# TensorE's products as one loop of seven passes behind an empty pass, with GpSimd passing on its waits

## Chip, cores and metric

The kernel runs on one NeuronCore of a Trainium2 chip. The metric is the device time of one execution in microseconds; the median of the runs shown is given, and durations of single steps come from one profiled execution.

## What is computed

One decoding step for 8 sequences: layer norm, attention with 32 query heads over 4 key/value heads, where only the last 1024 of 4096 cached positions count, a residual, a second layer norm and a gated feed-forward block, all in float32.

```python
def reference(A_x, A_k_cache, A_v_cache, A_wq, A_wo, B_x, B_w_gate, B_w_up, B_w_down):
    # x (8,1,1024), wq (1024,4096), k/v_cache (8,4,4096,128), wo (4096,1024)
    q = heads(layernorm(x) @ wq)                 # 32 heads of 128
    k, v = the last W = 1024 rows of the caches, each head for 8 query heads
    p = softmax(q k^T * 128 ** -0.5)
    h = x + heads_joined(p v) @ wo
    g, u = layernorm(h) @ w_gate, layernorm(h) @ w_up      # (8,1,3584)
    return h + (gelu(g) * u) @ w_down                      # w_down (3584,1024)
```

All weights and the used part of the caches are read once, some 111 MB; there are only 8 rows of activations, so each number that is read takes part in 8 products per head or token.

## The kernel before

Each stage streams its operand from HBM into one of two SBUF buffers of 64 KB per partition (`space`, two times `BUF`) and TensorE multiplies the small activations (stationary, 32 columns) with 512 columns of it at a time. Four such products stand next to each other on the array, one per group of 32 columns, and are summed in PSUM over the steps of the contraction. The loads follow each other on SyncE's queue in a fixed order: `wq` (two of 8 MB), the keys (two), the values (two), `wo` (two), gate and up in a first set of 2048 columns (two of 8 MB) and a second of 1536 columns (two of 6 MB), then `w_down`, 28 blocks of 128 rows in parts of 8, 8, 4, 4, 2 and 1 blocks (`PARTS`), the last block in two halves (`ENDS`). A load waits until the products on the buffer's last content are done (`free`, `used`), and is then queued behind the load that is still running.

`Flow.run` puts one instruction on an engine with the waits that it needs and lets it count up the engine's semaphore; `Flow.move` issues one DMA with a semaphore of its own; a wait that the engine has already made is left out. Every program line is unrolled: 479 matrix products and transposes are written out one after the other (helper lines L192 for transposes, L237 `wq`, L265 scores, L312 values, L340 `wo`, L351 the fold of four partial sums, L380 gate and up, L466 and L489 to L501 `w_down`).

Between two products stand VectorE's and ScalarE's steps: scale and transpose of q (L243, L248), softmax (L274 to L279), the weighting of the heads (L319, L322), residual and second layer norm (L354, L202 to L223), gelu and product (L390, L393). From block 19 of `w_down` the last 296 columns (`SIDE_COLS`) are not moved with their part but by eight small DMAs of four rows each into a tile of their own, `w_side` (L440), and multiplied by L476.

The end: `d1` (L480) copies the sum of all but the last two blocks out of PSUM, L489 multiplies block 26 and folds `d1`, L501 multiplies the two halves of block 27 as they land, ScalarE copies each half (L504), and two DMAs write the output.

## Time and profile before

| | |
|---|---|
| median of 3 runs | 265.19 us (265.16 to 265.31) |
| span of the profiled execution, first to last instruction | 264.1 us |
| what lies around the span, by the median | 1.1 us |
| TensorE busy with products | 142.2 us (54%) |
| TensorE instructions (products and weight loads) | 958 and 958 |
| moved by DMA | 111.4 MB, mean 422 GB/s |
| of it, code of the engines | 8 packets, some 0.12 MB |
| mean granted TensorE clock | 0.793 |

The page puts the busy shares of the engines first, then the span in 40 slices, the DMA queues, and the chain of work that ended last. A queue of the kind "instruction" moves an engine's own program. In the views by window the DMA share is the mean busy share of the 16 DMA engines; a packet is counted where it starts, so that in windows shorter than a packet the share tells how many packets start there, and at the end of the kernel, where packets are short, how many of the 16 engines are still busy.

### The profile page before, as it was taken

What the parts mean: (1) busy time and instruction counts of PE and PEld (TensorE: products, weight loads), DVE (VectorE), ACT (ScalarE), POOL (GpSimd) and SP (SyncE); (2) the same over time, 40 slices, a digit from 0 to 9 for tenths busy, and PEclk for the clock granted to TensorE, in tenths of its full rate; (3) what the DMA queues carried; (4) which work ended last, traced back from release to release, by engine and by line L of the source; (5) the groups of instructions that cost most, each with busy time, mean ns of one, the idle gap of its engine ahead of it and who ended that gap; (6) DMA issues with size and microseconds to landing.
All of it is one profiled execution on the core that took longest, in us unless ns stands there. A gap on an engine that the chain in (4) does not pass through costs nothing.

```text
span 264.1 us, 2072 instructions
## 1 busy us (share of the span) xinstructions
PE 142.2 (54%) x958; PEld 40.9 (15%) x958; DVE 23.3 (9%) x55; ACT 10.9 (4%) x17; POOL 5.5 (2%) x15
## 2 busy tenths in 40 slices
PE   0006905905905906907807507818609477589875
PEld 0002201201201301302202102212102111113122
DVE  0040000000020110110110100170000200000001
ACT  1020000000010020020000000020000000000000
POOL 8000000000000000000000000000000000000000
PEclk9999985865875975985956965975957959599999
DMA  8998999999899989999998999899998999999994
GB/s 318 481 437 357 476 476 390 407 466 466 347 466 466 459 347 466 459 407 417 447 466 367 469 437 466 377 447 457 429 419 387 476 402 427 417 462 409 410 413 181
DMA packets 3256, 111.44 MB, mean 422 GB/s; under 512 B 392, under 2 KB 648, under 8 KB 1072
## 3 DMA queue, kind: packets, MB, share of 16 engines
q1 hardware_dynamic: 3088, 111.22, 97.9%
q8 instruction: 7, 0.11, 0.2%
q10 hardware_dynamic: 160, 0.10, 0.1%
q14 instruction: 1, 0.01, 0.0%
HBM read 111.18 MB, written 0.13 MB: 421 GB/s over the span
## 4 chain that ended last, share of the span: by engine, by line
DMA 78%; PE 21%; SPq 0%; issue 0%; ACT 0%
DMA w<-gu 20%; DMA w<-wq 16%; DMA w<-v 11%; DMA w<-kt 11%; DMA w<-wo 11%; DMA w<-dn 9%; PE big L380 6%; PE tb L312 4%; PE tb L237 4%; PE ya L340 3%; PE big L265 3%; SPq L91 0%; PE acc L489 0%; ACT o_fin L504 0%; PE tb L489 0%
## 5 line engine op out<-in xcount | busy, mean ns | idle before, releaser
L380 PE MATMUL big<-w,ln_t 128*32 128x512 f32 x224 | 37.7, 752 | 19.8 <-DMA w<-gu 19.8
L265 PE MATMUL big<-w,qz 128*32 128x512 f32 x128 | 18.8, 753 | 18.3 <-DMA w<-kt 18.3
L340 PE MATMUL ya<-w,ot 128*32 128x512 f32 x128 | 17.9, 721 | 19.9 <-DMA w<-wo 19.9
L466 PE MATMUL ya<-w,at 128*32 128x512 f32 (+1 forms) x104 | 16.4, 591 | 3.2 <-DMA w<-dn 3.2
L380 PEld LDWEIGHTS big<-w,ln_t 128*32 128x32 f32 x224 | 9.2, 134 | 46.9 <-issue 24.9
L192 PE MATMUL ta<-ident,ln_xn 64*128 64x64 f32 x16 | 2.2, 318 | 24.4 <-DVE ln_xn L218 24.4
L312 PE MATMUL tb<-w,pt 128*32 128x512 f32 x64 | 9.9, 787 | 9.0 <-DMA w<-v 9.0
L312 PE MATMUL acc<-w,pt 128*32 128x512 f32 x64 | 9.4, 751 | 9.5 <-DMA w<-v 9.5
L237 PE MATMUL tb<-w,ln_t 128*32 128x512 f32 x64 | 9.8, 783 | 8.6 <-DMA w<-wq 8.6
L237 PE MATMUL acc<-w,ln_t 128*32 128x512 f32 x64 | 9.2, 742 | 2.6 <-DMA w<-wq 2.6
L340 PEld LDWEIGHTS ya<-w,ot 128*32 128x32 f32 x128 | 4.8, 128 | 31.5 <-issue 31.5
L265 PEld LDWEIGHTS big<-w,qz 128*32 128x32 f32 x128 | 4.8, 134 | 31.6 <-issue 22.5
L466 PEld LDWEIGHTS ya<-w,at 128*32 128x32 f32 x104 | 4.2, 109 | 15.0 <-issue 10.6
L393 DVE TENSOR_TENSOR hm<-ge,big 128x512 f32<-128x512 f32 (+1 forms) x2 | 1.4, 684 | 56.6 <-PE big L380 56.6
L192 PEld LDWEIGHTS ta<-ident,ln_xn 64*128 64x128 f32 x16 | 1.8, 216 | 25.3 <-DVE ln_xn L218 25.3
L274 DVE TENSOR_REDUCE nmax<-big 128x1 f32<-128x1024 f32 x2 | 2.4, 1224 | 33.8 <-PE big L265 33.8
L276 ACT ACTIVATE p<-big,nmax 128x1024 f32<-128x1024 f32 x2 | 2.2, 1113 | 71.9 <-DVE nmax L274 71.9
L312 PEld LDWEIGHTS tb<-w,pt 128*32 128x32 f32 x64 | 2.6, 139 | 15.6 <-issue 15.6
L312 PEld LDWEIGHTS acc<-w,pt 128*32 128x32 f32 x64 | 2.5, 135 | 15.7 <-issue 15.7
L237 PEld LDWEIGHTS tb<-w,ln_t 128*32 128x32 f32 x64 | 2.3, 139 | 15.4 <-DMA w<-wq 8.8
L237 PEld LDWEIGHTS acc<-w,ln_t 128*32 128x32 f32 x64 | 2.5, 134 | 8.6 <-issue 8.6
L209 ACT ACTIVATE ln_sd<-ln_ve 64x1 f32<-64x1 f32 x2 | 0.4, 203 | 73.9 <-DVE ln_ve L208 73.9
(81 smaller groups left out, 53.1 us busy)
## 6 DMA issues: line engine op xcount, KB each, us to landing
w<-gu SPq DMA_DIRECT2D x2, 6144.0 KB, 23.9
w<-dn SPq DMA_DIRECT2D x2, 4096.0 KB, 27.0
w<-dn SPq DMA_DIRECT2D x1, 2048.0 KB, 19.6
w<-dn SPq DMA_DIRECT2D x1, 1900.0 KB, 23.3
w<-dn SPq DMA_DIRECT2D x1, 1024.0 KB, 21.7
w<-dn SPq DMA_DIRECT2D x1, 512.0 KB, 22.5
w<-ends SPq DMA_DIRECT2D x2, 256.0 KB, 22.7
w_side<-side SPq DMA_DIRECT2D x8, 18.5 KB
```

The costliest lines, as they stand in the source:

```text
L192: tok = run("tensor", lambda e, i=i: e.transpose(t[:, i, :], src[:, i * P:(i + 1) * P], ident[:rows, :rows]), id_ok, ready, clear, mark=(i ...
L209: tok = run("scalar", lambda e: e.activation(sd, ve, AF.Sqrt), tok)
L237: tok = run("tensor", lambda e, c=c, j=j: e.matmul(q_ps[32 * j:32 * j + 32, :], xt[c], w[:, c, j * N:(j + 1) * N], start=(c == 0), stop=(c ...
L265: tok = run("tensor", lambda e: e.matmul(s_ps[32 * r:32 * r + 32, k0:k0 + N], qz[hf][:, s, c0:c0 + 32], k_t[:, s, half * HB + b, k0:k0 + N ...
L274: tok = run("vector", lambda e: e.tensor_reduce(out=nmax, in_=s_ps, axis=AX.X, op=ALU.max, negate=True), tok)
L276: p_ok = run("scalar", lambda e: e.activation(p_sb, s_ps, AF.Exp, bias=nmax, accum_out=tot), tok)
L312: tok = run("tensor", lambda e: e.matmul(o3[32 * r:32 * r + 32], pt[:, c, 32 * r:32 * r + 32], v_t[:, s, c, half * HB:(half + 1) * HB, :], ...
L340: tok = run("tensor", lambda e: e.matmul(ya[32 * r:32 * r + 32, :], ot[:, 2 * hf * REP + h + e2].rearrange("p r b -> p (r b)"), w[:, h + e ...
L380: tok = run("tensor", lambda e: e.matmul(pair[32 * j:32 * j + 32, s, :], ht[c], w[:, c, j * N:(j + 1) * N], start=(c == 0), stop=(c == NC ...
L393: tok = run("vector", lambda e: e.tensor_mul(hm[:rows], ge[:rows], pair[:rows, 1, :]), tok, g_ok)
L466: tok = run("tensor", lambda e: e.matmul(ya[32 * r:32 * r + 32, 0:n], at[:, q + e2, :], rows_of(q + e2)[:, ch * N:ch * N + n], start=(r no ...
```

## The change

All of TensorE's large products become one loop of seven passes (`nc.Fori`, on TensorE alone). For this every stage gets one shape: 16 loads, again in two buffers of 64 KB per partition, each with 8 steps of four products (`STEPS`, `products`). One pass holds eight transposes of `xs[1]` (`turn`), the products on buffer 0, eight transposes of `xs[0]`, the products on buffer 1, and in pass 3 alone the fold and a copy of the residual. The seventh pass has only its first half. The counter begins at -1: in that pass a branch skips the whole body, to the loop's end, and from there the loop goes back to its head.

Within the loop TensorE waits for one semaphore only, `go`: GpSimd makes all waits in TensorE's order and counts `go` up once for each, and TensorE counts it down. Only the products behind the loop wait for themselves. The sums of the first and last four steps go to two PSUM banks and are added by VectorE or ScalarE. The second set of gate and up has 1536 columns; the free fourth column group of its loads takes the first 8 blocks of `w_down`, so that these two loads are 8 MB too (the second of them in two halves). 16 blocks of `w_down` follow in three DMAs (4, 2 and 2 steps), then two blocks (`pair`), one (`single`) and the last in two halves, as before. The side tile `w_side`, its eight DMAs and its products are gone, and x comes with one DMA instead of two.

The diff, cut (VectorE's and ScalarE's steps between the products are left out where they only follow the new shapes):

```diff
-PARTS = (8, 8, 4, 4, 2, 1)
-SIDE = 19
...
+STEPS = 8
+LOAD = STEPS * NQ * N
+PASSES = 7
+WO, GU0, GU1, DN = 3, 4, 5, 6
+CUTS = (0, 4, 6, STEPS)
+LAST = DF // P - 1
+EARLY = 8
...
-    for b in range(0, B, HB):
-        fl.start("scalar", lambda e: e.dma_start(
-            x_sb[b * STEP:(b + HB) * STEP:STEP, :], x[b:b + HB]), [x_zero]).then_inc(x_in, 16)
...
+    landed = {(0, 0): [move("w_0_0", buf[0], w[0])]}
+    x_in = move("x", x_sb[0:ROWS:STEP, :], x, x_zero, engine="scalar")
+    landed[0, 1] = [move("w_0_1", buf[1], w[1])]
+    for k in range(1, DN):
+        for s in range(2):
+            n = 2 * k + s
+            free = pe(f"{'ab'[s]}{k - 1}")
+            if (k, s) == (GU1, 1):
...
+            else:
+                landed[k, s] = [move(f"w_{k}_{s}", buf[s], w[n], free)]
+    landed[DN, 0] = [
+        move(f"wd{i}", buf[0][:, a * NQ * N:b * NQ * N], dn[i], pe(f"a{GU1}"))
+        for i, (a, b) in enumerate(zip(CUTS, CUTS[1:]))]
+    w_pair = buf[1][:, 0:NQ * N]
+    pair_in = move("wp", w_pair, pair, pe(f"b{GU1}"))
...
-    w_side = sb("w_side", 64, len(SIDE_ROWS), SIDE_COLS)
...
+    for s, h in enumerate("ab"):
+        need[f"{h}3"] = [*landed[WO, s], *st_ok[s], *o_free[s]]
...
+    need["fold"] = [tok, consts]
+    h_ok = run("vector", lambda e: e.tensor_add(
+        h_sb[0:ROWS], x_sb, fin[0:ROWS]), pe("fold"), clear[2])
+    need["res"] = [h_ok]
...
+    ready = layernorm(h_sb[0:ROWS], xs[1], h_ok, "ln2", pe("tb2"))
+    need["tb3"] = [ready, *tt_free]
+    st_ok = [(t,) for t in tokens_in([pe("tb3")])]
...
-    d1_ok = run("vector", lambda e: e.tensor_copy(d1, ya), tok)
+    tok = run("vector", lambda e: e.tensor_add(d1, ob[0][:, 0:N], d0), pe(f"a{DN}h"), d0_ok, ex_ok)
...
+    d1_ok = run("vector", lambda e: e.tensor_add(d1, ob[0][:, N:2 * N], d1), pair_done, tok)
...
+    for name in pe_waits():
+        left = fl.missing("gpsimd", need.pop(name, []))
+        for s, v in left[:-1]:
+            nc.gpsimd.wait_ge(s, v)
+        if left:
+            nc.gpsimd.wait_ge(*left[-1]).then_inc(go, 1)
+        else:
+            nc.gpsimd.sem_inc(go, 1)
...
+    def wait():
+        nc.tensor.wait_ge(go, 1).then_inc(go, -1)
...
+    def turn(src):
+        for i in range(NC):
+            ins = nc.tensor.transpose(t8[:, i, :], src[:, i * P:(i + 1) * P], ident)
+        marked(ins)
+
+    def products(s, cuts):
+        for i in range(STEPS):
+            if i in cuts:
+                wait()
+            for r in range(NQ):
+                c = i // (STEPS // 2) * N
+                ins = nc.tensor.matmul(
+                    ob[s][32 * r:32 * r + 32, c:c + N], st[s][:, i * P + 32 * r:i * P + 32 * r + 32],
+                    buf[s][:, (i * NQ + r) * N:(i * NQ + r + 1) * N],
+                    start=(i % (STEPS // 2) == 0), stop=(i % (STEPS // 2) == STEPS // 2 - 1))
+            if i % (STEPS // 2) == STEPS // 2 - 1:
+                marked(ins)
+
+    with nc.Fori(-1, PASSES, engines=[mybir.EngineType.PE]) as it:
+        with nc.tensor.If(it >= 0):
+            wait()
+            turn(xs[1])
+            products(0, CUTS)
+            with nc.tensor.If(it < DN):
+                wait()
+                turn(xs[0])
+                products(1, (0, STEPS // 2))
+                with nc.tensor.If(it == WO):
+                    wait()
+                    for ch in range(2):
+                        ins = nc.tensor.matmul(
+                            fin[0:ROWS, ch * N:(ch + 1) * N], to_rows[:, ch, :], y_sb,
+                            start=True, stop=True)
+                    marked(ins)
...
+    first = LAST - 3
+    for i in range(NQ):
+        ch, e2 = divmod(i, 2)
+        tok = run("tensor", lambda e: e.matmul(
+            ob[0][32 * i:32 * i + 32, N:2 * N], at[:, first + e2, :], w_pair[:, i * N:(i + 1) * N],
+            start=False, stop=True, skip_group_check=True), pair_in, at_ok, mark=(i == NQ - 1))
...
+    add(lambda j: at[:, LAST - 1, :], lambda j: w_single[:, j * QW:(j + 1) * QW], single_in, res_ok,
+        start=True)
+    add(lambda j: add2[:, j // 2, :], lambda j: d1[:, (j % 2) * QW:(j % 2) * QW + QW], d1_ok)
```

## Rows read from the trace of the kernel before

**Rows 1.** The page: span, and shares of the chain that ended last

```profile
span 264.1 us, 2072 instructions
...
DMA 78%; PE 21%; SPq 0%; issue 0%; ACT 0%
```

**Rows 2.** Window: busy us (count) of PE, PEld, DVE, ACT, POOL; clock; DMA share; GB/s

```profile
59.80:79.20 19.40, 10.01 (x64) 2.36 (x64) 1.62 (x3) 1.20 (x2) 0.00 (x0) 0.68 1.00 432
```

**Rows 3.** Chain in order of time, a stretch: start us, us, what

```profile
42.43 9.89 PE tb L237 x64
...
52.33 29.55 DMA w<-kt
```

**Rows 4.** Waits of TensorE: who for whom, us in total, times, longest us

```profile
PE tb L237 <- DMA w<-wq: 8.6, 1, 8.6
```

**Rows 5.** DMA queues, whole span: packets, MB, share of 16 engines; one issue

```profile
q1 hardware_dynamic: 3088, 111.22, 97.9%
q8 instruction: 7, 0.11, 0.2%
...
q14 instruction: 1, 0.01, 0.0%
...
w_side<-side SPq DMA_DIRECT2D x8, 18.5 KB
```

**Rows 6.** DMA queues, windows 0 to 44 us (all its queues), then 46 to 47 us

```profile
q1 hardware_dynamic: 316, 18.61, 99.4%
q10 hardware_dynamic: 16, 0.03, 0.2%
...
q8 instruction: 1, 0.02, 6.5%
```

**Rows 7.** Windows at the end of the loads (columns as in rows 2)

```profile
258.00:259.00 1.00, 0.56 (x8) 0.00 (x0) 0.00 (x0) 0.00 (x0) 0.00 (x0) 1.00 1.03 406
259.00:261.20 2.20, 1.89 (x32) 0.72 (x36) 0.75 (x2) 0.00 (x0) 0.00 (x0) 1.00 0.55 210
259.20:260.40 1.20, 1.02 (x12) 0.12 (x12) 0.13 (x1) 0.00 (x0) 0.00 (x0) 1.00 0.70 270
...
260.80:261.00 0.20, 0.20 (x9) 0.00 (x0) 0.16 (x1) 0.00 (x0) 0.00 (x0) 1.00 0.14 51
261.00:261.20 0.20, 0.20 (x12) 0.18 (x12) 0.06 (x1) 0.00 (x0) 0.00 (x0) 1.00 0.03 10
```

**Rows 8.** Windows in which the second packet of each DMA engine starts

```profile
4.70:4.90 0.20, 0.00 (x0) 0.00 (x0) 0.00 (x0) 0.12 (x1) 0.20 (x1) 1.00 0.76 328
4.90:5.10 0.20, 0.00 (x0) 0.00 (x0) 0.00 (x0) 0.00 (x0) 0.20 (x1) 1.00 6.05 2621
5.10:5.30 0.20, 0.00 (x0) 0.00 (x0) 0.00 (x0) 0.00 (x0) 0.20 (x2) 1.00 3.78 1638
5.30:5.50 0.20, 0.00 (x0) 0.00 (x0) 0.00 (x0) 0.00 (x0) 0.20 (x2) 1.00 1.51 655
```

**Rows 9.** Groups by line and shape: count, busy us, mean ns, idle before

```profile
L380 PE MATMUL big<-w,ln_t 128*32 128x512 f32 x224 | 37.7, 752 | 19.8 <-DMA w<-gu 19.8
L192 PE MATMUL ta<-ident,ln_xn 64*128 64x64 f32 x16 | 2.2, 318 | 24.4 <-DVE ln_xn L218 24.4
```

**Rows 10.** Timeline around the second layer norm: start us, us, what

```profile
169.06 0.69 DVE L348 COPY y_sb<-ya 128x512 f32<-128x512 f32 x1 [19.07 <-PE ya L340]
...
179.19 9.72 PE L380 MATMUL big<-w,ln_t 128*32 128x512 f32 x64 [1.30 <-DMA w<-gu]
```

**Rows 11.** Timeline of the end

```profile
259.14 1.07 PE L466 MATMUL ya<-w,at 128*32 128x512 f32 x8 [0.57 <-DMA w<-dn]
260.27 0.69 DVE L480 COPY d<-ya 128x512 f32<-128x512 f32 x1 [21.07 <-PE ya L466]
...
261.02 0.43 PE L489 MATMUL acc<-d,add 128*32 128x128 f32 x8
...
261.70 0.40 PE L501 MATMUL tb<-w,at 128*32 128x128 f32 x8
```

## The prediction, made before the change was run

> **What bounds the kernel now.** I read the page first. Of the chain that ended last 78% is DMA and 21% TensorE [rows 1], so the next question is whether the loads ever pause for TensorE. The windows of one load's length say no: the mean busy share of the 16 DMA engines is 1.00, at 432 GB/s, while TensorE is busy half the time, 10.01 of 19.40 us [rows 2]. The chain shows the pattern: products 9.89 us, then a load that takes 29.55 us from its issue, because it queues some 10 us behind the load that still runs [rows 3]. Between its stages TensorE waits for data, at least 8.6 us at a time [rows 4]. So the kernel lasts as long as its DMA engines have work, plus a short end, and TensorE may be slower by about 8 us in any half pass without cost.

> The reader should then look at how the loads end. From 258 to 259 us all 16 engines are busy (1.03). From 259.2 to 260.4 the share is 0.70, which is 11 of 16, and the last packets start before 261.2 (0.14, then 0.03) [rows 7]. So five engines run out some 1.2 to 1.9 us ahead of the others. Each row of a load goes to the engines evenly, so something else occupies eleven of them. The queue rows show what: seven packets of TensorE's own code, 16 KB each, in the queue "instruction" [rows 5], one of which takes 6.5% of 16 engine-microseconds, 1.04 us of one engine [rows 6]. And the side tile: eight DMAs of four rows, 18.5 KB each [rows 5], hence on four engines 8 x 18.5 / 4 = 37 KB, which at 432/16 = 27 GB/s is 1.37 us. Seven and four are eleven. I infer from this that the seven code packets fall on seven different engines and the side rows on the four others that are late.

> **The change part by part.** *Bytes of the loads.* The sum stays what it was: 12 loads of 8 MB, then 8, 1, 0.5 and 0.5 MB. The side tile's 8 x 18.5 = 148 KB goes back onto all 16 engines, 9.25 KB or 0.34 us each, and leaves the four, 1.37 us.

> *TensorE's code.* A product of the program is two matmuls and two weight loads (224 matmuls for the 112 products of L380), a transpose one of each (16 for 16) [rows 9]. Now some 1,916 such instructions, with waits and branches more, bring seven packets, one for about each 270, and none in the first 44 us, whose queues show no code at all [rows 6]. So the first one or two stretches of code lie ready when the span begins. After the change the loop body has 64 products and 16 transposes, 64 x 4 + 16 x 2 = 288, the fold and residual 4 x 4 = 16, and some 20 waits and branches: about 325. Behind the loop stand 28 products, 112. That is some 440 in all, less than two stretches of 270. Whether a loop fetches its code again in each pass no row can show, since nothing branches here. The nearest row is the price of one packet, 1.04 us of one engine. The ends are zero packets within the loads, and some three in each pass (the far stretch, the head, the stretch behind the head), 21. I take zero or one, since the whole code fits into what two fetches bring, and the empty pass visits head and end once, in the first microsecond or two, before or just as the loads start. I keep the other end as a rival.

> *The sum.* Between 259.0 and 261.2 us the mean share is 0.55 [rows 7]: each engine idles 0.45 x 2.2 = 1.0 us in the mean, so the mean engine is through at 260.2. Without code it is through 7 x 1.04 / 16 = 0.46 us sooner, 259.75. The side tile doesn't change the mean. The engines start unevenly: of their second packets one starts before 4.9 us, eight before 5.1, five before 5.3 and two before 5.5 (a packet counts 0.756 in these windows) [rows 8], mean 5.1, last some 0.3 later. So the last engine would end at 260.05 instead of 261.15: 1.1 us less. The gap between early and late engines, up to 1.9 us where a packet explains 1.04, leaves room for 0.4 us more per code packet; then it would be 1.3. If one code packet still falls into the loads, on an engine that started early (0.3 before the mean), that engine ends at 259.75 - 0.3 + 1.04 to 1.4 = 260.5 to 260.85: 0.3 to 0.65 us less. The fetch of the empty pass falls where the first packets are just starting, so I take the middle of none and one, 0.8 us.

> *Longer chains on TensorE.* Eight transposes in every half pass, at 0.32 us each or less where they overlap [rows 9], add at most 2.5 us; a wait through GpSimd, a count up and a branch have no row, and the nearest is a semaphore step, from the last product (42.43 + 9.89 = 52.32) to the issue that waits for it at 52.33 [rows 3]. Even at fifty times that, 0.5 us each, nine waits and a few branches in a whole pass are some 6 us, of which half fall into either half pass, under the 8.6 us idle before the next load [rows 4]. What GpSimd holds is only these waits, in TensorE's order, behind its constants, which end at about 6 us; nobody else waits for it. The longest chain is the second layer norm: from the end of the `wo` products to the next products 10.1 us, 169.06 to 179.19 [rows 10]. Eight wide transposes and a copy four times as wide add 1.5 to 3 us. These products then end near 191 instead of 189 us; the load that waits for their buffer is wanted when the next one has landed, at about 198. So it is covered, and if the cover were gone, each microsecond over would be a microsecond of the total.

> *The end.* The block pair's products (1.07 us), the copy of the sum (0.69; the change adds out of PSUM instead, same width), the fold and the last block's products follow each other from 259.14 to the end with at most 0.57 us of idle in front [rows 11]. The order, the sizes and the direct waits stay, so the chain moves with its loads. TensorE leaves the loop while its last products still run. I count nothing, and 0 to +0.2 us for the range.

> [...]

> **The rivals.** *First, slower: code fetched in every pass.* [...] It is decided by whether the loop's two stretches stay while a third is fetched ahead. With up to 16 packets each engine has about one: 260.05 + 1.04 to 1.4, so 0 to 0.3 us more than now. With 21, five engines have two, 0.95 to 1.7 us more: 266.1 to 266.9, middle 266.4. For it: the kernel before fetches ahead at each stretch it enters, needed or not. Against it: the code needed is so little. The stalls themselves would hide in the idle of 8.6 us.

> *Second, the packets move and do not vanish.* One fetch per pass, or the programs of GpSimd and VectorE, which grow by half a hundred waits and two dozen steps; another engine's packet is 0.01 MB [rows 5], half the size. If such a packet falls on an engine that starts late (5.4 us), it ends at 260.05 + 0.5 to 1.4: between 0.6 less and 0.3 more, so 264.6 to 265.5, taken as 265.1. For it: one single packet late is enough to undo half the gain.

> **How the numbers follow.** Profiled span 264.1 us; less 0.8 is 263.3; around it lie 1.1 us, so 264.4. Its own range is 263.8 (1.3 us less) to 265.0 (0.2 less). Chances: 0.58 for the forecast, 0.14 for the second rival, 0.28 for the first, of which 0.20 are its costly form with 21 packets. A measurement here tells about 0.2%, 0.53 us. Faster by more, below 264.66: 0.49, all from the forecast. Within: 0.09 of the forecast, the second rival and the first with few packets, 0.31. Slower: 0.20. The range that leaves out no more than 0.2 runs from 263.8 over all cases but the costly one, to 266.0 with the bounds of the end and of the price of a packet.

> **What would show it.** Right: no code packet of TensorE's queue between 2 and 255 us, and a share in the last 2 us that falls from 1 to 0 within about 1 us, not in a step of 0.70. The first rival: 14 or more packets in that queue. The second: a few, and a single engine's tail in the share. Wrong altogether: a window with a DMA share under 0.95 in the middle, above all after the second layer norm, which would mean that a load waited for TensorE.

## The result, and the profile after

The kernel after takes 265.84 us (median of 20 runs, 265.30 to 267.66), the kernel before 265.27 us beside it (20 runs, 265.08 to 265.59). The ratio is 1.0029, with a 95% interval of 1.0017 to 1.0041: slower by 0.29% (by the medians alone 0.21%), where I forecast faster. Before, all runs lie within 0.5 us; after, within 2.4 us. The spans of the 20 executions and their mean granted clock go together:

```
after, span (us) / mean granted clock of TensorE
264.0 to 264.3   0.813 to 0.819   10 executions
264.7 to 265.6   0.806 to 0.807    7
266.0 to 266.3   0.801             3
```

The profiled execution is one of the short ones (265.30 us, span 264.0). Its page, span and the queues:

```profile
span 264.0 us, 2332 instructions
...
q1 hardware_dynamic: 3024, 111.22, 97.9%
q10 hardware_dynamic: 160, 0.10, 0.1%
q8 instruction: 1, 0.02, 0.0%
q14 instruction: 2, 0.02, 0.0%
```

In place of the seven packets of TensorE's code [rows 5] there is one: the loop of some 325 instructions goes round seven times and fetches nothing again. The queue of the other engines' code has two packets instead of one, both within the loads (169.6 and 250.5 us), where the one of before came behind them (262.3 us). The code packet of TensorE that is left lies here (queues of two windows):

```profile
q1 hardware_dynamic: 316, 18.61, 99.5%
q10 hardware_dynamic: 16, 0.03, 0.2%
q8 instruction: 1, 0.02, 0.1%
...
q1 hardware_dynamic: 7, 0.46, 529.2%
q8 instruction: 1, 0.02, 29.1%
```

The first three lines are of 0 to 44 us, where before had no code [rows 6]; the last two of 4.8 to 5.0 us. There seven of the engines start their second packet of data, just as in [rows 8], and 29.1% of 16 x 0.2 us is 0.93 us of one engine. So the fetch of the empty pass (without that pass the packet came at 48.7 us, experiment 4) comes when the loads have begun. The windows of one load's length and of the end of the loads (columns as in [rows 2]):

```profile
59.80:79.20 19.40, 10.16 (x72) 3.35 (x72) 2.31 (x4) 1.79 (x3) 0.00 (x0) 0.76 1.00 432
...
253.40:256.80 3.40, 0.42 (x8) 0.19 (x8) 0.00 (x0) 0.00 (x0) 0.00 (x0) 1.00 0.97 406
256.80:260.20 3.40, 2.69 (x24) 0.50 (x17) 0.07 (x1) 0.00 (x0) 0.00 (x0) 1.00 0.85 332
258.00:259.00 1.00, 0.48 (x8) 0.09 (x8) 0.00 (x0) 0.00 (x0) 0.00 (x0) 1.00 1.00 385
259.00:261.20 2.20, 1.97 (x36) 0.82 (x40) 0.69 (x2) 0.00 (x0) 0.00 (x0) 1.00 0.36 133
259.20:260.40 1.20, 0.98 (x16) 0.20 (x12) 0.26 (x1) 0.00 (x0) 0.00 (x0) 1.00 0.45 166
260.40:261.20 0.80, 0.79 (x28) 0.52 (x24) 0.43 (x2) 0.00 (x0) 0.00 (x0) 1.00 0.05 18
```

DMA is as full as before in the middle. At the end the mean share from 259.0 to 261.2 falls from 0.55 [rows 7] to 0.36: the mean engine is through 0.42 us sooner. But not all are. By the landings of the last load that every engine reports, thirteen engines are through by 260.4 and three at 260.9, 261.0 and 261.35; before, five by 259.7 and eleven from 260.9 to 261.6. Three code packets, three late engines. Which engine carried which packet the trace doesn't show, but the counts fit in other profiles too: nine packets and nine late engines in experiments 2, 7, 10 and 14, eight and eight in 3. Between these two profiles the last of all gains 0.25 us. The end of the kernel (timeline, start and length in us, in brackets the idle time in front and what ended it):

```profile
256.50 1.92 PE L442 MATMUL o<-w,st 128*32 128x512 f32 x16 [2.98 <-PEq L426]
258.94 1.06 PE L476 MATMUL o<-w,at 128*32 128x512 f32 x8 [0.52 <-DMA w<-ends]
260.23 0.64 PE L485 MATMUL fin<-w,at 128*32 128x128 f32 x16 [0.22 <-DMA w<-ends]
```

L476 is the pair's product, the L466 line of [rows 11]. It starts at 258.94 instead of 259.14, and from there to the end of the span 5.05 us pass, before 4.99. So this execution is 0.2 us earlier at the pair and 0.14 us shorter than the profiled one of before (263.99 and 264.13 us).

That is no gain of the change. The ten short executions take 265.41 us in the median, 0.14 us more than the median before. And in the profile of experiment 5, whose loads and seven code packets are those of the kernel before, the pair lands at 258.83 us and the last load at 261.35 us; in after it is 258.81 and 261.35. So 0.25 us is what two executions with the same loads differ by. The short executions show no gain, and the other half carries the loss. One such execution is the profile of the experiment that runs the same kernel again (span 265.0); first its timeline, then its windows. The trace counts matmuls, two for each product of the program:

```profile
256.59 3.54 PE L442 MATMUL o<-w,st 128*32 128x512 f32 x16 [2.98 <-PEq L426]
259.83 1.24 PE L476 MATMUL o<-w,at 128*32 128x512 f32 x8
260.86 0.65 PE L485 MATMUL fin<-w,at 128*32 128x128 f32 x16
261.94 0.64 PE L485 MATMUL fin<-d,add 128*32 128x128 f32 x16 [0.44 <-DVE mark L398]
```

```profile
253.40:256.80 3.40, 0.42 (x8) 0.19 (x8) 0.00 (x0) 0.00 (x0) 0.00 (x0) 0.99 0.94 394
256.80:260.20 3.40, 3.40 (x20) 1.06 (x16) 0.00 (x0) 0.00 (x0) 0.00 (x0) 0.51 0.85 331
```

The same sixteen matmuls (eight products) take 3.54 us instead of 1.92. The granted clock, sixth figure behind the length, is 0.51 from 256.8 to 260.2, where the short execution has 1.00; DMA is no slower (0.85 in both). Ahead of it TensorE was busy for 0.42 of 3.40 us; in the short execution, too, and there the clock stayed at 1.00. The three longest executions (266.0 to 266.3) were not profiled. The kernel before, in the same window and, below it, in its timeline:

```profile
253.40:256.80 3.40, 2.47 (x19) 0.67 (x18) 0.00 (x0) 0.00 (x0) 0.00 (x0) 1.00 0.97 401
```

```profile
239.42 7.04 PE L466 MATMUL ya<-w,at 128*32 128x512 f32 x32
246.95 3.64 PE L466 MATMUL ya<-w,at 128*32 128x512 f32 x32 [0.49 <-DMA w<-dn]
251.83 2.77 PE L466 MATMUL ya<-w,at 128*32 128x512 f32 x16 [1.24 <-DMA w<-dn]
```

It is busy for 2.47 us there. Ten blocks (`SLOW`: 0 to 7, 16, 17) go to two column groups instead of four: 32 matmuls take 7.04 us in the first line, 3.64 in the second, which has all four groups; the third has both kinds, and the side tile's products follow it. The change drops `SLOW`, since in the loop every product has its own group.

### The profile page after: what moved, and what is told of

Read it like the earlier page. It is cut to its first block, busy times and chain, and to the rows that moved or that the text cites. A ratio compares the mean times of both kernels' runs of the same rounds, so it can differ in the third digit from the quotient of the medians.

```text
span 264.0 us, 2332 instructions
## 1 busy us (share of the span) xinstructions
PE 139.1 (53%) x1000; PEld 47.6 (18%) x1000; DVE 40.0 (15%) x84; ACT 18.3 (7%) x27; POOL 5.5 (2%) x15
## 5 line engine op out<-in xcount | busy, mean ns | idle before, releaser
L442 PE MATMUL o<-w,st 128*32 128x512 f32 x832 | 117.0, 722 | 86.0 <-PEq L426 79.5
L442 PEld LDWEIGHTS o<-w,st 128*32 128x32 f32 x832 | 32.3, 130 | 162.5 <-issue 162.5
L433 PE MATMUL tt<-ident,xs 128*128 128x128 f32 x104 | 16.5, 311 | 33.6 <-PEq L426 33.6
L433 PEld LDWEIGHTS tt<-ident,xs 128*128 128x128 f32 x104 | 13.3, 160 | 44.0 <-issue 44.0
L272 DVE TENSOR_REDUCE nmax<-o 128x1 f32<-128x1024 f32 x2 | 2.4, 1224 | 32.6 <-PE o L442 32.6
L298 DVE SCALAR_TENSOR_TENSOR xs<-o,share,xs 128x128 f32<-128x128 f32 x14 | 4.9, 351 | 4.3 <-PE o L442 3.8
L274 ACT ACTIVATE xs<-o,nmax 128x1024 f32<-128x1024 f32 x2 | 2.2, 1114 | 39.5 <-DVE nmax L272 39.5
L363 DVE TENSOR_TENSOR u<-ge,o 128x512 f32<-128x512 f32 x2 | 1.4, 689 | 16.6 <-PE o L442 16.6
L364 DVE TENSOR_TENSOR u<-ge,o 128x512 f32<-128x512 f32 x2 | 1.4, 688 | 13.6 <-PE o L442 13.6
L235 DVE COPY st<-tt 128x1024 f32<-128x1024 f32 x2 | 2.4, 1224 | 4.3 <-PE tt L433 4.3
L305 DVE COPY st<-tt 128x512 f32<-128x512 f32 x4 | 2.6, 686 | 2.6 <-PE tt L433 2.6
```

The source lines that it names most:

```text
L235: a = run("vector", lambda e: e.tensor_copy(st[0].rearrange("p (c r b) -> p c r b", c=NC, b=B), xt.unsqueeze(2).to_broadcast([P, NC, P // ...
L272: tok = run("vector", lambda e: e.tensor_reduce(out=nmax, in_=ob[s], axis=AX.X, op=ALU.max, negate=True), pe(f"{h}1"))
L274: tok = run("scalar", lambda e: e.activation(xs[s], ob[s], AF.Exp, bias=nmax, accum_out=tot), tok)
L298: tok = run("vector", lambda e: e.scalar_tensor_tensor(out, o3[:, b], sh[:, b:b + 1], out, op0=ALU.mult, op1=ALU.add), tok, ready)
L305: tok = run("vector", lambda e: e.tensor_copy(heads[:, g], turned.unsqueeze(2).to_broadcast([P, REP, P // 2 // B, B])), pe(f"t{h}2"))
L433: ins = nc.tensor.transpose(t8[:, i, :], src[:, i * P:(i + 1) * P], ident)
```

## The experiments

All ratios are to the kernel before, run on the same chips (its medians 265.24 to 265.34). "Spans" are those of the single executions. The theories are: *clock* (the dropped `SLOW` lets the clock be at half at the end in some executions), *packets* (where the code packets fall) and *relay* (GpSimd passing on the waits costs time). The quoted texts number them, each text for itself.

**1. Three zero products between steps 4 to 5 and 6 to 7 of the first half.** Their stationary matrix is zero, so they add nothing to the sums.

```diff
+            if (s, i) == (0, CUTS[2]):
+                for _ in range(3):
+                    nc.tensor.matmul(ob[0][:, N:2 * N], zero, buf[0][:, 0:N], start=False, stop=False, ...)
```

> In every pass three products with a zero stationary matrix (128 columns, so they add nothing) stand between steps 6 and 7 of the first half; in the last pass they fill some 2.6 of the 3 us for which TensorE waits for the last two steps of w_down. Theory 1 (the changed kernel's long executions, up to 267.7 us at a granted clock of 0.801 to 0.807, have the low clock in the last 10 us, where TensorE idles more than before): the long executions go, median 265.2 to 265.4, spans 263.9 to 264.2, granted clock 0.82 or more. Theory 2 (the loop fetches code again in some executions): nothing changes, median 265.8, spans up to 266.

Measured 267.27 us, ratio 1.0068 (1.0051 to 1.0085), spans 264.7 to 266.6. The clock stayed at 1.00 until the output, but in the profile (span 266.6) a new code packet came with the output; that the twelve instructions more brought it there is my guess, and not shown. In two of the six executions, moreover, 2.2 us lie around the span instead of 1.3. DMA from 261 us on, queue and issues:

```profile
q8 instruction: 1, 0.02, 1.3%
...
out<-o_fin SPq DMA_DIRECT2D x1, 64.0 KB, 3.5
out<-o_fin ACTq DMA_DIRECT2D x1, 64.0 KB, 3.5
```

The output lands after 3.5 us instead of 1.6 (before and after). So this run holds the clock and pays 1.9 us elsewhere; it decides nothing about the price of the clock.

**2 and 3. All passes written out, with the relay and without it.**

```diff
-    with nc.Fori(-1, PASSES, engines=[mybir.EngineType.PE]) as it:
-        with nc.tensor.If(it >= 0):
+    for it in range(PASSES):
...
-        nc.tensor.wait_ge(go, 1).then_inc(go, -1)
+        for s, v in fl.missing("tensor", need.pop(order.pop(0), [])):
+            nc.tensor.wait_ge(s, v)
```

The first change alone is the first of the two kernels, both together the second.

> The seven passes written out, no loop and no empty pass; GpSimd still relays the waits. Theory 1 (clock at the end): the long executions stay, median 265.7 to 266.2. Theory 2 (code fetched again): they go, median about 265.4. By the balance of the DMA engines: 8 code packets instead of 1, one per engine, so the fast executions' span grows by 0 to 0.6 us over 264.0. If the 0.27 us that the changed kernel lasts longer outside its span (265.3 - 264.0 against 265.2 - 264.1) come from the loop, they go; if from the relayed waits or the new loads, they stay.

> The passes written out as in e2_unrolled, and TensorE makes its waits itself, without GpSimd. If the relay costs nothing on the path: same as e2_unrolled within 0.1 us. If the relay is late at the end: 0.2 to 0.5 us less. Outside the span 1.05 us if the relay (some 90 instructions on GpSimd) was the cause of 1.33.

Measured 266.65 us (ratio 1.0044, 1.0031 to 1.0057; spans 264.5 to 265.5) and 266.57 us (1.0040, 1.0024 to 1.0055; 264.2 to 266.3). The long executions stay without the loop and without the relay. The relay's price doesn't show in the times, which here tell no less than some 0.6 us. The traces show it: the products of the last two steps start 0.05 us behind the landing of their load when TensorE waits itself, and 0.18 us behind it with the relay. It is small beside the 2.98 us of idle in front. Without the loop there are eight packets of TensorE's code again, and from 260.4 to 261.2 us, where after has a share of 0.05 and before 0.25, the loads still run at 0.41 (the unrolled kernel's window):

```profile
260.40:261.20 0.80, 0.80 (x16) 0.21 (x12) 0.00 (x0) 0.00 (x0) 0.00 (x0) 1.00 0.41 156
```

The profile without relay had a code packet with the output, as in experiment 1 (landing 3.6 us); its clock was 1.00 until then. That of the unrolled kernel had the clock at half from 256.9 to 260.3 us.

**4. The loop without its empty pass.** `nc.Fori(0, PASSES)` and no first branch.

> The loop from pass 0, without the empty pass. If the loop's code stays resident and only the stretch behind it is fetched ahead, one code packet of TensorE's queue remains and comes near 30 us instead of 4.9 us; it delays one engine by 1.0 to 1.5 us as now: fast spans 264.0 to 264.4. If the empty pass is what makes the loop resident: several packets, spans 264.4 to 266.

Measured 266.29 us, ratio 1.0039 (1.0026 to 1.0052), spans 264.8 to 265.1. One code packet of TensorE too, but at 48.7 us, in the middle of the loads. The empty pass therefore removes no packet; it moves the one. All five executions had a mean clock of 0.806 to 0.813, and the profile shows the half clock at the end, so the price of the later packet can't be read from this run.

**5. The kernel before without its long products.**

```diff
-SLOW = (*range(0, 8), 16, 17)
+SLOW = ()
```

> The kernel before with SLOW = (): the products of blocks 0 to 7, 16 and 17 of w_down use all four column groups at once instead of two, so they take half the time and TensorE idles more in the last 25 us. Theory 1 (TensorE's activity in the last 25 us sets the clock at the end, and these slow products held it up): the kernel before now has long executions too, spans from 263.9 to 265.5 and more, median 265.5 to 266.3. Theory 2 (the long executions come from the loop, the relay or the new loads): no change, median 265.3, all spans within 263.7 to 264.3.

Measured 265.80 us, ratio 1.0014 (1.0005 to 1.0023), spans 263.8 to 264.9, six of eleven at 264.4 or more. One line of the kernel before gives it long executions, if not the longest of after (264.9 against 266.3). Its profile (span 264.8), timeline and window:

```profile
256.39 4.48 PE L466 MATMUL ya<-w,at 128*32 128x512 f32 x24 [1.31 <-DMA w<-dn]
```

```profile
256.80:260.20 3.40, 3.40 (x24) 0.77 (x20) 0.00 (x0) 0.00 (x0) 0.00 (x0) 0.56 0.89 354
```

The 24 matmuls of 256.39 took 1.92 + 1.07 = 2.99 us before; here 4.48, at a clock of 0.56. Ahead of them TensorE idled for 1.31 us only and was busy for 2.09 of 3.40 us (253.4 to 256.8), more than in either execution of after.

**6 and 7. Another order of issue.** In steps 0 to 5 of the first half the products of two steps are issued column group by column group, so that neighbours share a group; as a loop and written out.

```diff
+            steps = [(i0 + e, r) for e in range(2) for r in range(NQ)]
+            if s == 0 and i0 < CUTS[2]:
+                steps = [(i0 + e, r) for r in range(NQ) for e in range(2)]
```

> The changed kernel; in the first half of every pass the products of steps 0 to 5 are issued two steps of one column group behind each other instead of four groups side by side, so that they overlap less and take longer; no instruction is added. Theory 1: the long executions go, all spans 263.9 to 264.3, median 265.3 to 265.45. Theory 2: spread stays, median 265.8.

> As e6_slowed, with the passes written out: 8 code packets instead of 1. With the clock out of the way this is what the loop is worth. By the landings of the last load (261.35 us with the loop, 261.81 without): 0.3 to 0.6 us more than e6_slowed, median 265.7 to 265.9. If the loop is worth nothing: the same.

Measured 266.55 us (1.0044, 1.0030 to 1.0058; spans 263.9 to 266.3) and 266.59 us (1.0039, 1.0023 to 1.0055; 264.4 to 265.9). The edit did not do what it was meant to: 32 matmuls took 3.68 us, in after 3.64. So the order of issue did not make products long here; with two of the four groups empty 32 matmuls took 7.04 us in the kernel before. The spread stays, as the clock theory says of products that are not long. What the pair gives is the loop's worth in short executions: the shortest spans are 263.9 with the loop and 264.4 without.

**8. The kernel after once more.**

> The changed kernel once more on this chip, for its spread beside the others and a profile that may be one of a long execution. Theory 1: in a long execution the granted clock falls to 0.5 somewhere from 253 us on, the products of the last steps take 3.4 instead of 1.9 us, and the queue of TensorE's code still has one packet before 255 us. Theory 2: more code packets.

Measured 265.99 us, ratio 1.0020 (1.0009 to 1.0032), spans 264.0 to 265.1. Its profile is the long execution shown above. Its mean clock, 0.813, is that of some short ones: the mean over the span doesn't tell what the clock was at the end.

**9 and 10. Two zero products instead of three, as a loop and written out.**

> As e1_warm with two of the added products in a pass instead of three, 1.9 us, so that TensorE's code may end before the next stretch of code (in e1_warm a code packet at 263.9 us held up one engine's part of the output by 1.9 us). Theory 1 (the clock at the end): if no code packet falls on the output, all spans 263.9 to 264.3 and the median 265.25 to 265.5, with a granted clock over 0.82. If the packet still comes: spans up to 266.5 again. Theory 2: spread as in the changed kernel, median 265.9.

> e9_warm2 with the passes written out: 8 code packets or more instead of 1, with the clock held up as there. What the loop is worth alone. By the balance of the engines 0.3 to 0.6 us more than e9_warm2; if the loop is worth nothing, the same.

Measured 266.39 us (1.0044, 1.0023 to 1.0064; spans 263.8 to 266.2) and 266.16 us (1.0041, 1.0026 to 1.0056; spans 264.2 to 266.5). In both profiles the clock is 1.00 until the products are done. But long executions remain, and here the clock doesn't explain them: 266.2 at a mean of 0.820, beside 263.8 at 0.819. In three executions of the first, moreover, 2.6 to 2.8 us lie around the span instead of 1.3. Both profiles are of short executions, so the cause stays open; that the added code moved a packet to the end in the long ones is my guess, and not shown. The runs speak against the clock as the only source of spread in a kernel with these products.

**11. Balancing the end.** With two zero products; 432 columns of the single block go in 16 DMAs of eight rows into a tile of their own, behind the pair.

```diff
+    for p0 in range(0, P, 8):
+        fl.start("sync", lambda e: e.dma_start(
+            w_single[p0:p0 + 8, 0:SHIFT], single[p0:p0 + 8, 0:SHIFT]), []).then_inc(side_in, 16)
```

> e9_warm2, and 432 of the 1024 columns of the block behind the pair move in 16 DMAs of 8 rows, which are expected on 8 of the 16 engines; each of these has 13.5 KB (0.5 us) more than before, each other 13.5 KB less. If the engine that takes TensorE's code packet is the last one now (261.35 us against 260.4 for most) and not among the 8: the last landing 0.4 to 0.5 us earlier, median 264.8 to 265.1. If it is among them: 0.5 us later.

Measured 268.14 us, ratio 1.0101 (1.0086 to 1.0116). The small DMAs filled the engines worse (258 to 259 us: share 1.06, but 228 GB/s, after 385), the single block's products started only at 262.58, and by then the clock was at half. This edit failed as built; it says nothing about balance as such.

**12 and 13. Long products again, at the end.** The loop has six passes, the half pass stands written out behind it. In the first kernel steps 4 and 5 use two column groups; the second is its control.

```diff
-            for r in range(NQ):
+            for r in ((0, 2, 1, 3) if i in slow else range(NQ)):
+                g = r // 2 * 2 if i in slow else r
...
-    with nc.Fori(-1, PASSES, engines=[mybir.EngineType.PE]) as it:
+    with nc.Fori(-1, DN, engines=[mybir.EngineType.PE]) as it:
...
+    wait()
+    turn(xs[1])
+    products(0, CUTS, (4, 5))
```

> The loop has six passes; the seventh, half pass stands written out behind it, and there the products of steps 4 and 5 (blocks 16 to 19 of w_down) use two column groups instead of four, so that they take about 3.6 us instead of 1.9 and TensorE idles about 1.3 us instead of 3 before the last two steps. Nothing is added and nothing left out. Theory 1 (the change lost time because it dropped the double-length products, so that in some executions the granted clock is at half before the end): all spans lie within 0.3 us of each other, near 264.0 as the kernel before, median time 265.3 to 265.4, whatever the mean clock. Theory 2 (the spread of the changed kernel comes from something else at the end, as the kernel with two zero products suggests, where spans up to 266.2 came with a clock no lower than that of the short ones): spans spread from 264.0 to 266 as before, median 265.8 or more. Theory 3 (code: the half pass behind the loop is some 150 instructions more, so one or two packets more): the shortest span rises to 264.3 to 264.6 and stays constant.

> As the kernel with the half pass behind a loop of six passes, but with four column groups in steps 4 and 5 as in the changed kernel: the control. Theory 1: spans from 264.0 to 266 as in the changed kernel, median 265.8 or more, the longer ones at a lower mean clock. Theory 2: the same. Theory 3: the same shift of the shortest span as in its partner. If both partners have constant spans, the loop's seventh pass was the cause, and not the products' length.

Measured 265.57 us (1.0015, 1.0006 to 1.0024; spans 264.0 to 264.6) with the long products and 266.20 us (1.0027, 1.0017 to 1.0037; spans 264.1 to 265.6) without. Nothing was added, and the two differ in the length of eight products (sixteen matmuls). First the timeline with long products (span 264.0) and its windows, then those of the control (span 265.6):

```profile
246.74 8.76 PE L444 MATMUL o<-w,st 128*32 128x512 f32 x48 [1.89 <-PEq L426]
256.52 1.92 PE L444 MATMUL o<-w,st 128*32 128x512 f32 x16 [1.02 <-PEq L426]
258.97 1.06 PE L481 MATMUL o<-w,at 128*32 128x512 f32 x8 [0.52 <-DMA w<-ends]
```

```profile
253.40:256.80 3.40, 2.38 (x14) 0.64 (x14) 0.00 (x0) 0.00 (x0) 0.00 (x0) 1.00 0.96 402
257.80:261.20 3.40, 2.65 (x44) 0.89 (x40) 0.69 (x2) 0.00 (x0) 0.00 (x0) 1.00 0.59 223
```

```profile
247.26 7.05 PE L442 MATMUL o<-w,st 128*32 128x512 f32 x48 [1.76 <-PEq L426]
257.07 3.18 PE L442 MATMUL o<-w,st 128*32 128x512 f32 x16 [2.75 <-PEq L426]
259.69 1.98 PE L478 MATMUL o<-w,at 128*32 128x512 f32 x8
```

```profile
253.40:256.80 3.40, 0.92 (x12) 0.01 (x2) 0.02 (x1) 0.00 (x0) 0.00 (x0) 1.00 0.96 405
257.80:261.20 3.40, 3.40 (x21) 1.38 (x16) 0.00 (x0) 0.00 (x0) 0.00 (x0) 0.51 0.69 266
```

TensorE idles 1.02 us in one and 2.75 us in the other ahead of the last two steps; then the clock is 1.00 in one and 0.51 in the other, where the half level covers the pair's products too (1.98 us instead of 1.06). In both it was at half once before, from about 247 to 251 us. The clock theory had asked for spans within 0.3 us and got 0.6, against 1.5 of the control: right in kind, not complete. The intervals of the two ratios overlap a little; the means of the runs differ by 0.49 us, and only the control has spans above 264.6. Neither is faster than the kernel before.

**14. All written out, with the long products.** Steps 4 and 5 of the last half pass on two groups, no loop.

> All passes written out, as in the unrolled kernel, and in the last half pass steps 4 and 5 on two column groups. Theory 1: spans constant within 0.3 us, near 264.5 (eight code packets), median 265.8, where the unrolled kernel spread from 264.5 to 265.5. The difference between this and the loop with the same slow steps is then the worth of the loop alone, about 0.5 us. Theory 2: a spread as in the unrolled kernel.

Measured 265.86 us, ratio 1.0023 (1.0013 to 1.0033), spans 264.2 to 264.8, as constant as those of 12. The loop with the same products took 265.57: with the end held, the loop alone is worth 0.29 us against the same kernel written out. The pair's products start at 259.51 us here and at 258.97 there, and the span ends 5.1 and 5.0 us later.

## Why the prediction was wrong

**The bound: right.** The DMA share is 1.00 at 432 GB/s in the window of one load, after as before [rows 2], and from 100 to 242 us it is nowhere under 0.97 in windows of some 20 us. (In windows of 10 us it swings, 0.94 beside 1.09, since a packet counts where it starts.)

**No code fetched per pass: right.** One packet of TensorE's code in after and in experiments 4, 6, 8, 9 and 11; one more behind the loop in 1, 12 and 13. The first rival's case, code fetched in every pass, did not occur here, though its sign came true: there was one packet in seven passes with a body of some 325 instructions. What spoke for it is in the trace of the kernel before: the seven packets start between 46.05 and 255.22 us, the first of them while the products of [rows 3] run on (42.43 to 52.32 us), the last with only 145 of the 1,916 instructions still to start.

**0.8 us from the packets: this step failed first, at "I take the middle of none and one".** The one packet came at 4.9 us, when the first data packets were already running, and the second rival's other programs brought two packets into the loads, where before had none. The middle of two outcomes was no outcome. My mean of the engines held: the share fell by 0.42 us per engine where I had 0.46. The split into seven late engines and four fits the landings too: eleven late ones. But the last landing is that of the slowest engine, and one is late whether seven packets are left or one. Between the two profiles it came 0.25 us sooner, and in experiment 5 the loads of before landed as early as those of after. Even the case with one packet, "0.3 to 0.65 us less", was too much. The short executions (265.3 to 265.6) are nearest to the second rival, 265.1 us, and not below the time before.

Against the same kernel written out the loop is worth something: the last load lands at 261.7 to 261.9 us in the five profiles without it (experiments 2, 3, 7, 10, 14) and at 261.2 to 261.6 in most with it (261.9 and 262.1 in 13 and 1; 11 has other loads). But the loads of the kernel before, with the side tile and seven packets, end at 261.60 and, in experiment 5, at 261.35. So the rest of the change takes back what the loop gives; which part does is not shown.

**Which landing counts: not seen.** I moved the whole end with the last landing. It isn't waited for: the last half block's products start 0.46 us behind the fold (L485 on `d`) in the short execution and 0.47 in the long one, where the last landing is 1.0 us back. In every profile with the clock held and no code packet in the output, the span ends 5.0 to 5.1 us after the pair's products start. But the pair's landing doesn't decide alone. The chain that ended last goes through the single block's, in after and, below, before:

```profile
243.00 17.09 DMA w<-ends
260.23 0.64 PE fin L485 x16
260.88 0.64 PE fin L485 x16
```

```profile
237.88 22.46 DMA w<-dn
260.38 0.43 PE acc L489 x8
```

In after the single block's products end at 260.87 us and VectorE's sum of the pair at 260.82; the fold waits for both. So two landings count within 0.05 us of each other, and neither is the last.

**"I count nothing, and 0 to +0.2 us for the range" for the end: this step failed too, and it made the loss.** I wrote that order, sizes and direct waits stay, and passed over a line of the diff that I had in hand, `r = ch if q in SLOW else i`, whose loss makes the products in front of the end half as long (3.64 us for 32 matmuls instead of 7.04). It showed in the rows: the clock stands as 1.00 in [rows 7], and I never asked what kept it there while the page's mean was 0.793. The same products then ran at half the clock in part of the executions: 3.54 us instead of 1.92, and a span 1.0 us longer (265.0 against 264.0). Removing `SLOW` alone costs the kernel before 0.5 us in the median (experiment 5), putting long products back gains 0.63 us in the median (12 against 13), both close to the 0.57 us that the change lost. In the kernel before the executions differ in their mean clock too, 0.78 to 0.83, and their spans don't: elsewhere a slow TensorE hides in the idle of 8.6 us [rows 4]; at the end nothing hides it. That TensorE leaves the loop while its last products still run came true (last branch at 257.0 us, products to 258.42).

**Around the span: 1.1 us was too little.** It is 1.3 us, before and after. I had set the median of the runs against the span of an execution that was some 0.2 us longer than the median one; the pair of the same execution was needed. 264.4 should have been 264.6 by my own sum.

**Longer chains: right.** From the end of the `wo` products to the products behind the second layer norm 13.5 us pass (168.0 to 181.54), before 10.1 [rows 10]; I had added 1.5 to 3, and it is 3.4. "At least 8.6 us" of idle was read from one row: ahead of the second set of gate and up TensorE waited for 4.4 and 4.6 us only, which did no harm. They end at 190.97, I had said 191, and the window from 190 to 200 us has a DMA share of 0.98. The relay adds some 0.13 us to a wait (experiments 2 and 3), and the loads stay full.

**What stays open.** What decides in a given execution whether the clock falls is not shown: the same idle led to either level. The parts don't quite close: the unrolled program with the end held is 0.6 us slower than the kernel before (265.86 to 265.24), of which the loop gives 0.3 back. That rest is likely the side tile, eight packets instead of seven and the longer programs of the others; I haven't parted them. Nor do I know the cause of the spread of 0.6 us in experiment 12, and of that of the kernels with zero products.

## What to carry over

When a kernel is bound by DMA, sum what the slowest of the 16 engines carries up to the landing that the last chain waits for, and not the mean or the number of packets: six of seven code packets went and the slowest engine gained 0.25 us at most. In the last microseconds TensorE is on the critical path too (here the 5.0 us from the pair's products on), so ask of each line that a change drops whether the clock at the end is lower without it: products twice as long as needed cost nothing in front of a wait here (265.57 us in experiment 12, 266.20 in its control), and half the clock behind it cost a microsecond (span 265.0 against 264.0 us). A median with a wide spread asks for the long execution's profile as well as the short one's, and a gain of 0.2 us between two profiles for a second profile of the same kernel.
